# A level found in five digits of the logits' range instead of eight digits of their bits

## The chip, the core and the metric

The kernel runs on one core of one Trainium2 chip. The metric is the device time of one execution in microseconds, the median of the runs. The core has TensorE (PE, matmuls), VectorE (DVE), ScalarE (ACT), GpSimd (POOL) and SyncE (SP); each runs its own list of instructions in order and waits for the others by semaphores.

## What is computed

A gated linear recurrence, then a mixture of eight experts with balanced assignment. The reference, cut:

```python
# attention: B=4, H=8, S=768, D=48
f = 1.0 / (1.0 + np.exp(-f_logit))
for t in range(S):
    state = f[:, :, t, :, None] * state + np.einsum('bhd,bhe->bhde', k[:, :, t], v[:, :, t])
    y[:, :, t] = np.einsum('bhd,bhde->bhe', q[:, :, t], state)
# experts: x is (3072, 384), E=8, F=1024
cap = N // E                                   # 384
logits = x @ w_gate
order = np.argsort(-logits.flatten())
for idx in order:                              # the largest logit first
    tok, e = idx // E, idx % E
    if assigned[tok] >= 0 or counts[e] >= cap: continue
    assigned[tok] = e; counts[e] += 1
for e in range(E):
    mask = assigned == e
    out[mask] = np.maximum(x[mask] @ w1[e], 0.0) @ w2[e]
```

## The kernel before

**Attention.** 24 chunks of 128 positions pass through seven stages (loads and decays, gates, states, scores, outputs, transposition, gate), one chunk per stage and step. In each step DVE clips the decays (`dl`), makes `qg`, masks the scores (`am`, two predicated copies), copies `kT`, `xT` and the chunk's `logits`; POOL makes `kg`; PE's Y of a step reads the `am` of the step before. A scheduler sets the order of this part. The rows x go to `xd` in DRAM.

**Routing.** `assign_and_run` writes its order out by hand for all engines but SP. The assignment is found in seven rounds. In each, every free token takes its best open expert (`choices`: `masked`, `best`, `pick`, `taken`, `choice`), and the round looks for the highest level at which an open expert fills up. The level is searched in digits of 16 values: DVE compares each token's remainder `over` with 15 thresholds (`above`), PE counts tokens by expert and threshold (`cnt`), DVE finds the thresholds at which an expert is full (`fills`, `filled`), PE sums the digit times its unit back over all partitions, and DVE subtracts it (new `over`). The key is the logit's 32 bits in sortable form, in two halves: four digits on the high half (`high_keys`), then four on the low one (`low_keys`), with an operation between that joins them. Then `assign` takes all tokens above the level (`sure`) and, of those exactly at it (`tie`), the first ones in token order, by two more matmuls, a scan and a rank. `close` marks full experts (`penalty`, `wanted`). Each round fills an expert, and its list is made (`members`, `place`, `index`, `lines`, six `in_line`, `used`, `tokens`: twelve operations in a queue `dve_work`): `index` gives the expert's number `e` to SP, which loads its weights, and `tokens` the rows that POOL gathers from `xd` (`xe`).

**Experts.** An expert is 51 pieces of PE work in a queue `pe_work`: three `turn` (the transpositions `Xe`, copied by ACT to `xeT`), 24 `up` (`H`, with a Relu by ACT to `hT`) and 24 `down` (`O`); each finished O tile is copied by ACT and scattered to the output by POOL. `some(pe_work, n)` puts n pieces at this place of PE's order. In a search the three numbers of `pace` are the pieces ahead of the count, of the sum over groups, and of the digit's matmul: none in round 0, where there is nothing to run, (1, 1, 1) in rounds 1 and 2, (2, 1, 1) after. In rounds 1 and 2 the whole list is made right after the assignment, with one piece behind each operation; later the operations of a list are put into the next round's digits, three in each, at the places of `some(dve_work, 1)`. In round 0 `idle_turns` runs empty matmuls (`nothing`). What is left in the queue at the end runs without a break.

**A second pass.** `beyond` counts spans too long for the fast attention; every engine loads it into a register at the end, behind the last list, and if it is over zero attention and routing run once more in a slower form.

## Time and profile before

| | us |
|---|---|
| median of 3 runs | 557.81 |
| lowest and highest run | 557.68 and 567.76 |
| the profiled execution | 559.02 |
| its span | 557.1 |
| PE busy | 497.1 (89%) |
| DVE busy | 292.8 (53%) |
| ACT and POOL busy | 128.4 (23%) and 114.4 (21%) |

The span is the time from the first to the last instruction of the profiled execution. A matmul in fp32 shows as two passes in the trace, so a piece of an expert is two rows. A timeline row joins equal instructions in a row; what stands in brackets is the idle time of the engine just before and what ended it. Attention fills the first 168 us, round 0 goes on to about 209, and PE ends at 547.4.

### The profile page before, as it was taken

Reading aid. Unit: us, or ns where it says so; the run is one execution under the profiler, and the core shown is the slowest. Engines: PE = TensorE matmul, PEld = TensorE weight load, DVE = VectorE, ACT = ScalarE, POOL = GpSimd, SP = SyncE. Lnnn points to the kernel's source line nnn. Section 1 sums busy time; section 2 is a strip of 40 time slices with the busy share of each in tenths; the row PEclk is TensorE's granted clock in tenths of the full one; section 3 lists DMA queues with packets and bytes.
Section 4 is the critical chain, followed back from the end, with each engine's and each line's share of the span. In section 5 each row is a group of like instructions: output and inputs, shape, how many; then the busy total and the mean of one; then the engine's idle time right before and its main releaser. Section 6 shows DMA issues by size and latency. Waiting matters only on the chain.

```text
span 557.1 us, 12270 instructions
## 1 busy us (share of the span) xinstructions
PE 497.1 (89%) x5054; PEld 310.7 (56%) x5054; DVE 292.8 (53%) x990; ACT 128.4 (23%) x301; POOL 114.4 (21%) x172
## 2 busy tenths in 40 slices
PE   3999999999993489998997989889899989999993
PEld 2778888878873254453353545445455556556551
DVE  6566566566665664575576477377576673000000
ACT  3445554544320001101111110210111021121210
POOL 3224433422310020041013003203112143101001
PEclk9999999999995599998999999899989999999997
DMA  9878898952100070061053007107125087100000
GB/s 176 180 159 172 186 190 192 195 129 60 45 34 14 1 270 0 1 252 59 1 196 105 11 0 256 57 2 254 58 66 203 29 282 276 38 1 28 14 16 32
DMA packets 118353, 59.10 MB, mean 106 GB/s; under 512 B 101648, under 2 KB 112912, under 8 KB 118288
## 3 DMA queue, kind: packets, MB, share of 16 engines
q1 hardware_dynamic: 111760, 44.06, 29.9%
q0 software_dynamic: 3072, 9.44, 5.1%
q10 hardware_dynamic: 3456, 4.72, 2.4%
q8 instruction: 42, 0.69, 0.5%
q14 instruction: 23, 0.19, 0.1%
HBM read 48.77 MB, written 9.44 MB: 104 GB/s over the span
## 4 chain that ended last, share of the span: by engine, by line
PE 64%; issue 18%; DVE 11%; POOL 4%; DMA 1%; ACT 1%; POOLq 0%; ACTq 0%; DVEq 0%
PE H L697 17%; PE O L708 14%; PE Y L239 4%; PE T L185 4%; PE A L222 3%; PE L L153 3%; PE Y L249 2%; PE L L157 2%; PE X L265 2%; PE dS L204 2%; PE cnt L501 2%; POOL out_dram L713 2%; PE X L279 1%; PE nothing L729 1%; DMA xe<-xd,token 1%
## 5 line engine op out<-in xcount | busy, mean ns | idle before, releaser
L697 PE MATMUL H<-xeT,w 128*128 128x384 f32 x384 | 150.5, 520 | 4.2 <-ACT xeT L689 4.2
L708 PE MATMUL O<-w,hT 128*128 128x384 f32 x384 | 140.7, 504 | 0.0
L697 PEld LDWEIGHTS H<-xeT,w 128*128 128x128 f32 x384 | 68.3, 196 | 39.5 <-ACT xeT L689 5.5
L708 PEld LDWEIGHTS O<-w,hT 128*128 128x128 f32 x384 | 68.4, 191 | 36.5 <-issue 1.1
L701 ACT ACTIVATE hT<-H 128x384 f32<-128x384 f32 x64 | 31.4, 490 | 137.7 <-PE H L697 130.1
L713 POOL DMA_INDIRECT out_dram<-o,token x24 | 24.5, 1020 | 184.8 <-ACT o L712 184.2
L227 DVE COPY_PREDICATED am<-mask,A 128x512 f32<-128x512 int32 x48 | 32.4, 728 | 31.5 <-PE A L222 31.5
L712 ACT COPY o<-O 128x384 f32<-128x384 f32 x24 | 11.5, 478 | 143.3 <-PE O L708 138.0
L383 DVE TENSOR_TENSOR in_line<-line,count 128x512 bf16<-128x512 f32 x48 | 32.2, 711 | 0.2
L663 POOL DMA_INDIRECT xe<-xd,token x24 | 24.1, 1006 | 38.3 <-DVE over L383 12.9
L177 POOL TENSOR_TENSOR kg<-k,ek 128x384 f32<-128x384 f32 x24 | 25.5, 1063 | 28.5 <-ACT ek L165 22.8
L501 PEld LDWEIGHTS <-above 128*120 128x120 bf16 x144 | 13.9, 135 | 29.0 <-DVE above L383 20.8
L153 PE MATMUL L<-g,wcum 128*128 128x384 f32 x48 | 23.0, 564 | 7.9 <-DVE count L322 7.9
L239 PE MATMUL Y<-v,am 128*64 128x48 f32 x768 | 27.7, 224 | 0.0
L383 DVE TENSOR_TENSOR above<-over,steps 128x360 bf16<-128x360 f32 x49 | 26.1, 533 | 1.7
L239 PEld LDWEIGHTS Y<-v,am 128*64 128x64 f32 x768 | 24.5, 138 | 4.1 <-issue 3.7
L222 PE MATMUL A<-qT,kT 48*64 48x128 f32 x768 | 26.7, 278 | 0.0
L383 DVE TENSOR_TENSOR own<-cnt,mine 120x64 f32<-120x64 f32 x48 | 10.7, 223 | 27.8 <-PE cnt L501 27.4
L162 DVE TENSOR_SCALAR dl<-L 128x384 f32<-128x384 f32 x24 | 13.4, 558 | 20.3 <-PE L L157 20.3
L629 POOL TENSOR_TENSOR past<-b,ramp_nt 128x48 f32<-128x48 f32 x8 | 2.2, 278 | 106.2 <-DVE b L383 81.0
L501 PE MATMUL cnt<-choice,above 128*120 128x64 bf16 x144 | 15.6, 218 | 8.5 <-DVE above L383 8.5
L689 ACT COPY xeT<-Xe 128x384 f32<-128x384 f32 x24 | 10.9, 486 | 47.3 <-PE Xe L686 45.3
(164 smaller groups left out, 639.5 us busy)
## 6 DMA issues: line engine op xcount, KB each, us to landing
w<-in_moe_w_dram SPq DMA_DIRECT2D x16, 1536.0 KB, 8.5
f<-in_f_logit_dram SPq DMA_DIRECT2D x24, 192.0 KB, 4.0
q<-in_q_dram SPq DMA_DIRECT2D x24, 192.0 KB, 3.9
k<-in_k_dram SPq DMA_DIRECT2D x24, 192.0 KB, 4.4
v<-in_v_dram SPq DMA_DIRECT2D x24, 192.0 KB, 3.9
xd<-x ACTq DMA_DIRECT2D x24, 192.0 KB, 3.3
xe<-xd,token POOLq DMA_INDIRECT x24, 3.1
out_dram<-o,token POOLq DMA_INDIRECT x24, 2.6
```

The source lines that it names most:

```text
L153: nc.tensor.matmul(out=Lv, lhsT=wcum[:], rhs=g[:, :, 0:DH], start=True, stop=True)
L177: nc.gpsimd.tensor_tensor(out=kg[:, :, 0:DH], in0=G["k"][:], in1=ek[:], op=ALU.mult)
L222: nc.tensor.matmul(out=A[par][HC * j:HC * j + HC, 128 * hp:128 * hp + 128], lhsT=G["kT"][rows, hp, HC * j:HC * j + HC], rhs=G["qT"][rows, ...
L227: nc.vector.copy_predicated(am[:, par], mask[:].unsqueeze(1).to_broadcast((128, HP, 128)), A[par][:].rearrange("s (a t) -> s a t", t=128))
L239: nc.tensor.matmul(out=Y[par][HC * j:HC * j + HC, DH * hp:DH * hp + DH], lhsT=G["am"][:, par, hp, HC * j:HC * j + HC], rhs=G["v"][:, 2 * h ...
L383: nc.vector.tensor_tensor(out=out_, in0=a, in1=b, op=op)
L501: nc.tensor.matmul(out=r[0:m, 0:n], lhsT=above[:, c:c + CG].rearrange("p c n -> p (c n)"), rhs=choice[:, c:c + CG].rearrange("p c e -> p ( ...
L663: nc.gpsimd.indirect_dma_start(out=xe[:], out_offset=None, in_=xd[:, :], in_offset=bass.IndirectOffsetOnAxis(ap=token[:, i:i + 1], axis=0))
L697: nc.tensor.matmul(out=L["H"][:, 0:CAP], lhsT=L["w1"][:, d, 128 * ft:128 * ft + 128], rhs=xT[:, d, :], start=(d == 0), stop=(d == DC - 1))
L701: nc.scalar.activation(out=hT[:, ft, :], in_=L["H"][:, 0:CAP], func=AF.Relu)
L708: nc.tensor.matmul(out=L["O"][:, 0:D], lhsT=hT[:, ft, 128 * i:128 * i + 128], rhs=L["w2"][:, ft, :], start=(ft == 0), stop=(ft == FC - 1))
L713: nc.gpsimd.indirect_dma_start(out=outs[next(tiles)][:, :], out_offset=bass.IndirectOffsetOnAxis(ap=L["token"][:, i:i + 1], axis=0), in_=o ...
```

## The change

The level is no longer searched in the logit's bits but in 2^20 equal steps. Near the end of attention `bounds` takes the largest and the smallest logit of the first four of six chunks of each sequence, widens the range by an eighth on either side and makes thresholds and units for five digits from its step. `level_keys` is one operation, the logit's distance from the lower end. A round has five digits. `assign` takes all tokens at or above the level, whole steps, with no ranking of ties. If a step holds more tokens than the expert has places, `places` falls below zero; `close` keeps the lowest (`lowest`), and at the end that too sets `beyond`. The old search with its ties runs only in the second pass, which makes its own constants. `pace` after round 2 becomes (3, 2, 2). A place of a list that stays empty points at 32 rows of zeros behind `xd` (the ramps are shifted by NT for that), and the scatter leaves out rows beyond N.

```diff
+SHIFTS = (16, 12, 8, 4, 0)
...
-    xd = dram.tile([N, D], FP32, name="xd")
+    xd = dram.tile([N + 32, D], FP32, name="xd")
+    zeros = const([32, D], FP32, "zeros")
+    nc.vector.memset(zeros[:], 0.0)
...
+    nc.scalar.dma_start(out=xd[N:N + 32, :], in_=zeros[:])
...
-    nc.gpsimd.iota(out=lane_i[:], pattern=[[1, 1]], base=0, channel_multiplier=1)
+    nc.gpsimd.iota(out=lane_i[:], pattern=[[1, 1]], base=-NT, channel_multiplier=1)
...
-    ramp_nt = ramp(NT, "ramp_nt", 1, -1)
+    ramp_nt = ramp(NT, "ramp_nt", 1, -1 - NT)
...
+    def bounds(c1):
+        pair = rt([2], "pair_", FP32, 1)
+        seen = logits[:].rearrange("p (b c) e -> p b c e", b=B)[:, :, 0:c1]
+        XY = mybir.AxisListType.XYZ
+        nc.vector.tensor_reduce(out=pair[:, 0:1], in_=seen, axis=XY, op=ALU.max)
+        nc.vector.tensor_reduce(out=pair[:, 1:2], in_=seen, axis=XY, op=ALU.min)
+        ts(pair[:, 1:2], pair[:, 1:2], -1.0, ALU.mult)
+        r = ps("bounds")
+        nc.tensor.transpose(out=r[0:2, 0:128], in_=pair[:], identity=ident[:])
+        top, tops = rt([1], "top", FP32, 1), rt([2], "tops", FP32, 1)
+        reduce(top[0:2, :], r[0:2, 0:128], ALU.max)
+        ts(tops[0:2, :], ident[0:2, 0:2], top[0:2, :], ALU.mult)
+        nc.tensor.matmul(out=r[:, 128:130], lhsT=two[0:2, :], rhs=tops[0:2, :], start=True,
+                         stop=True)
+        ends, width = rt([2], "ends", FP32, 1), rt([1], "width", FP32, 1)
+        nc.vector.tensor_copy(out=ends[:], in_=r[:, 128:130])
+        reduce(width[:], ends[:], ALU.add)
+        stt(lowlogit[:], width[:], -0.125, ends[:, 1:2], ALU.mult, ALU.subtract)
+        short, step = rt([1], "short", BF16, 1), rt([1], "step", FP32, 1)
+        ts(short[:], width[:], 1.25 / 2 ** 20, ALU.mult, 1e-30, ALU.max)
+        nc.vector.tensor_copy(out=step[:], in_=short[:])
+        for shift in SHIFTS:
+            steps = const([128, NTH], FP32, f"steps_{shift}")
+            ts(steps[:], count[:, 0:NTH], step[:], ALU.mult, float(1 << shift), ALU.mult)
+            unit = const([128, 128], BF16, f"unit_{shift}")
+            ts(unit[:], ones[:], step[:], ALU.mult, -float(1 << shift), ALU.mult)
+            digits.append((steps, unit))
+    def level_keys(best, over):
+        ts(over, best, lowlogit[:], ALU.max, lowlogit[:], ALU.subtract)
...
-            high_keys(best[:], of(key), half[:], of(high))
+            level_keys(best[:], of(over))
...
-        def search(choice, over, slots):
-            for shift, slots in zip((12, 8, 4, 0), slots):
+        def search(choice, over, digits, slots):
+            for steps, unit in digits:
...
         def assign(choice, over, slots):
+            sure = rt([NT, E], "sure", BF16)
+            stt(sure[:], col(over[:], E), 0.0, choice[:], ALU.is_ge, ALU.mult)
+            count = rt([E], "count", BF16)
+            with nc.allow_low_precision("counts of at most 24"):
+                reduce(count[:], by_e(sure), ALU.add)
+            some(pe_work, slots[0])
+            r = bank("sums", "r")
+            nc.tensor.matmul(out=r[:, 0:E], lhsT=ones[:], rhs=count[:], start=True, stop=True)
+            some(pe_work, slots[1])
+            tt(assigned[:], assigned[:], sure[:], ALU.add)
+            tt(places[:], places[:], r[:, 0:E], ALU.subtract)
+            ts(full[:], places[:], 0.5, ALU.is_lt)
+        def assign_exact(choice, over, slots):
+            after, notfirst, _ = exact
...
         def close():
             ts(penalty[:], full[:], CLOSED, ALU.mult)
+            tt(lowest[:], lowest[:], places[:], ALU.min)
...
-                nc.vector.tensor_copy(out=pair[:].rearrange("p a n -> p (a n)"), in_=r[:, 0:2 * TE])
+                ts(pair[:].rearrange("p a n -> p (a n)"), r[:, 0:2 * TE], float(NT), ALU.add)
...
-                            in_=o[:], in_offset=None)
+                            in_=o[:], in_offset=None, bounds_check=N - 1, oob_is_err=False)
...
-                low = rt([NT], "low")
-                low_keys(key[:], low[:])
-                slots = [pace.get(rnd, (2, 1, 1))] * 4
-                over = search(choice, high, slots)
-                stt(over[:], over[:], 65536.0, low[:], ALU.mult, ALU.add)
-                over = search(choice, over, slots)
+                slots = pace.get(rnd, (3, 2, 2))
...
+                        level_keys(best[:], over[:])
+                    over = search(choice, over, digits, slots)
...
             if again is not None:
+                worst = rt([1], "worst")
+                reduce(worst[:], lowest[:], ALU.min)
+                stt(beyond[:], worst[0:1, :], -0.5, beyond[:], ALU.is_lt, ALU.max)
                 again.append(nc.values_load(beyond[0:1, 0:1], min_val=0, max_val=128))
...
-    attention(6, ALL - 4)
+    attention(6, ALL - 8)
+    bounds(NCH - 2)
+    attention(ALL - 8, ALL - 4)
...
-        assign_and_run(None)
+        assign_and_run(exact=exact_constants())
```


**PE in round 3, from one digit's count to the next.** `cnt` are the search's matmuls, O the pieces of an expert, numbers in names the buffers. Before:

```order
L501 MATMUL cnt<-choice,above 120x64
L708 MATMUL O<-w_4009,hT 128x384
L513 LDWEIGHTS pick_th
L513 MATMUL cnt<-part,pick_th 15x8
L708 MATMUL O<-w_4009,hT 128x384
L535 LDWEIGHTS unit_538
L535 MATMUL cnt<-filled,unit_538 128x1
L708 MATMUL O<-w_4009,hT 128x384 x2
L501 LDWEIGHTS above
L501 MATMUL cnt<-choice,above 120x64
```

After:

```order
L551 MATMUL cnt<-choice,above 120x64
L775 MATMUL O<-w_3822,hT 128x384 x2
L563 LDWEIGHTS pick_th
L563 MATMUL cnt<-part,pick_th 15x8
L775 MATMUL O<-w_3822,hT 128x384 x2
L585 LDWEIGHTS unit_2666
L585 MATMUL cnt<-filled,unit_2666 128x1
L775 MATMUL O<-w_3822,hT 128x384 x3
L551 LDWEIGHTS above
L551 MATMUL cnt<-choice,above 120x64
```

Two pieces stand where one stood, and three where two stood, around the same search matmuls.

**DVE in the attention step in which the bounds are made**, from `dl` on. Before:

```order
L162 TENSOR_SCALAR dl<-L 128x384
L167 COPY spans<-L 128x8
L281 COPY logits<-X 128x8
L268 COPY xT<-X 128x384
L176 TENSOR_TENSOR qg_94<-q,eq 128x8x48
L227 COPY_PREDICATED am_99<-mask,A 128x512 x2
```

After:

```order
L170 TENSOR_SCALAR dl<-L 128x384
L175 COPY spans<-L 128x8
L406 TENSOR_REDUCE top<-bounds 2x1
L289 COPY logits<-X 128x8
L400 TENSOR_SCALAR tops<-ident,top 2x2
L184 TENSOR_TENSOR qg_96<-q,eq 128x8x48
L436 COPY ends<-bounds 128x2
L276 COPY xT<-X 128x384
L406 TENSOR_REDUCE width<-ends 128x1
L403 SCALAR_TENSOR_TENSOR lowlogit<-width,ends 128x1
L400 TENSOR_SCALAR short<-width 128x1
L442 CAST step<-short 128x1
```

Behind the last row shown follow `steps` and `unit`, five times each, and then the two `am` that closed the rows of before.

**PE at the end of round 4**, from the last digit's last count to the pieces ahead of the next round's first count. `Xe` are the transpositions of the gathered rows. Before:

```order
L513 MATMUL cnt<-part,pick_th 15x8
L697 MATMUL H<-xeT,w_4777 128x384
L535 LDWEIGHTS unit_546
L535 MATMUL cnt<-filled,unit_546 128x1
L549 LDWEIGHTS ones
L549 MATMUL sums<-tie,ones 128x192
L550 LDWEIGHTS after
L550 MATMUL sums<-tie,after 128x192
L697 MATMUL H<-xeT,w_4777 128x384
L557 LDWEIGHTS ones
L557 MATMUL sums<-count,ones 128x8
L697 MATMUL H<-xeT,w_4777 128x384 x10
```

After:

```order
L563 LDWEIGHTS pick_th
L563 MATMUL cnt<-part,pick_th 15x8
L775 MATMUL O<-w_4095,hT 128x384 x2
L585 LDWEIGHTS unit_2674
L585 MATMUL cnt<-filled,unit_2674 128x1
L753 MATMUL Xe<-ident,xe 128x128 x3
L602 LDWEIGHTS ones
L602 MATMUL sums<-count,ones 128x8
L753 MATMUL Xe<-ident,xe 128x128 x6
L764 MATMUL H<-xeT,w_4441 128x384 x9
```

The two `sums<-tie` are gone, and the transpositions of expert 3, which stood two digits earlier, now stand around the count's matmul.

## Rows read from the trace of the kernel before

**Rows 1.** The page, granted clock of PE in 40 slices of 13.9 us.

```profile
PEclk9999999999995599998999999899989999999997
```

**Rows 2.** Timeline of PE: start us, us, engine, line, operation, count [idle before, releaser].

```profile
481.26 1.15 PE L686 MATMUL Xe<-ident,xe 128*128 128x128 f32 x9
483.18 15.75 PE L697 MATMUL H<-xeT,w 128*128 128x384 f32 x48 [0.78 <-ACT xeT L689]
...
514.25 1.15 PE L686 MATMUL Xe<-ident,xe 128*128 128x128 f32 x9
```

**Rows 3.** Timeline of DVE, round 0.

```profile
171.61 0.18 DVE L383 TENSOR_TENSOR over<-high,cnt 128x24 f32<-128x24 f32 x1 [0.25 <-PE cnt L535]
...
173.78 0.18 DVE L383 TENSOR_TENSOR over<-over,cnt 128x24 f32<-128x24 f32 x1 [0.25 <-PE cnt L535]
...
187.30 0.36 DVE L390 SCALAR_TENSOR_TENSOR tie<-over,choice 128x192 bf16<-128x192 f32 x1
...
188.71 0.16 DVE L383 TENSOR_TENSOR places<-places,sums 128x8 f32<-128x8 f32 x1
...
191.31 0.16 DVE L383 TENSOR_TENSOR score<-left,full 128x8 f32<-128x8 f32 x1
```

**Rows 4.** Timeline of PE, two digits of round 1.

```profile
212.62 0.35 PE L501 MATMUL cnt<-choice,above 128*120 128x64 bf16 x3
...
215.59 0.35 PE L501 MATMUL cnt<-choice,above 128*120 128x64 bf16 x3
```

**Rows 5.** Timeline of PE, two digits of round 3.

```profile
317.44 0.30 PE L501 MATMUL cnt<-choice,above 128*120 128x64 bf16 x3
...
320.84 0.30 PE L501 MATMUL cnt<-choice,above 128*120 128x64 bf16 x3
```

**Rows 6.** The page, groups: line, engine, operation, busy us and mean ns, idle before.

```profile
L383 DVE TENSOR_TENSOR in_line<-line,count 128x512 bf16<-128x512 f32 x48 | 32.2, 711 | 0.2
```

**Rows 7.** Timeline of PE, end of round 2.

```profile
276.53 0.17 PE L535 MATMUL cnt<-filled,unit 15*128 15x1 bf16 x1
277.37 0.50 PE L549 MATMUL sums<-tie,ones 128*128 128x192 bf16 x1 [0.67 <-DVE tie L390]
...
278.72 4.12 PE L697 MATMUL H<-xeT,w 128*128 128x384 f32 x12
```

**Rows 8.** Timeline of PE, start of round 3.

```profile
296.90 0.35 PE L501 MATMUL cnt<-choice,above 128*120 128x64 bf16 x3 [2.94 <-DVE above L383]
```

**Rows 9.** Waits from 205 to 560: who waited for whom, us, times, longest.

```profile
PE cnt L501 <- DVE above L383: 8.5, 7, 3.6
...
PE cnt L513 <- DVE part L393: 1.9, 4, 0.7
```

**Rows 10.** Timeline of PE, round 4.

```profile
345.54 0.76 PE L653 MATMUL tokens<-number,in_line 128*128 128x6 bf16 x24
...
350.13 0.55 PE L686 MATMUL Xe<-ident,xe 128*128 128x128 f32 x3 [0.38 <-DMA xe<-xd,token]
...
357.51 0.30 PE L501 MATMUL cnt<-choice,above 128*120 128x64 bf16 x3
```

**Rows 11.** Timeline of PE, end of round 5 and start of round 6.

```profile
402.10 8.08 PE L697 MATMUL H<-xeT,w 128*128 128x384 f32 x15 [0.56 <-ACT xeT L689]
...
411.63 0.30 PE L501 MATMUL cnt<-choice,above 128*120 128x64 bf16 x3
```

**Rows 12.** Busy us of each engine in one stretch, granted clock.

```profile
402.00:405.00 3.00, 2.90 (x5) 1.68 (x6) 2.89 (x10) 0.05 (x1) 0.00 (x0) 0.50 0.02 5
```

**Rows 13.** Timeline of DVE, attention.

```profile
140.88 1.35 DVE L227 COPY_PREDICATED am<-mask,A 128x512 f32<-128x512 int32 x2 [1.56 <-PE A L222]
```

**Rows 14.** Timeline of PE, attention.

```profile
143.82 1.14 PE L239 MATMUL Y<-v,am 128*64 128x48 f32 x32
```

**Rows 15.** Timeline, last list: DVE's expert number and SP's DMA.

```profile
459.04 0.14 DVE L387 TENSOR_SCALAR e<-m 128x1 int32<-128x1 f32 x1
...
459.73 0.37 SPq L610 DMA_DIRECT2D w<-in_moe_w_dram  x1
```

More of the change, by code (lines that the diff above doesn't have):

```diff
@@ L309 @@
     nc.vector.memset(ones[:], 1.0)
-    after = const([128, 128], BF16, "after")
-    nc.vector.tensor_tensor(out=after[:], in0=ltri[:], in1=ones[:], op=ALU.subtract)
     onesf = const([128, 1], FP32, "onesf")
     nc.vector.memset(onesf[:], 1.0)
+    two = const([2, 128], FP32, "two")
+    nc.vector.memset(two[:], 1.0)
     onesc = const([128, NT], FP32, "onesc")
@@ L333 @@
     first = ramp(E, "first", -1, E + 1)
-    steps, units = {}, {}
-    for shift in (12, 8, 4, 0):
-        steps[shift] = ramp(NTH, f"steps{shift}", 1 << shift, 0)
-        units[shift] = const([128, 128], BF16, f"unit{shift}")
-        nc.vector.memset(units[shift][:], -float(1 << shift))
     mine8 = const([128, CG, E], FP32, "mine8")
@@ L359, with exact_constants @@
     nc.vector.memset(idle[:], 1.0)
-    notfirst = const([128, E, NT], FP32, "notfirst")
-    nc.vector.memset(notfirst[:], 1.0)
-    nc.vector.memset(notfirst[:, :, 0:1], 0.0)
+    def exact_constants():
+        after = const([128, 128], BF16, "after")
+        nc.vector.tensor_tensor(out=after[:], in0=ltri[:], in1=ones[:], op=ALU.subtract)
+        notfirst = const([128, E, NT], FP32, "notfirst")
+        nc.vector.memset(notfirst[:], 1.0)
+        nc.vector.memset(notfirst[:, :, 0:1], 0.0)
+        digits = []
+        for shift in (12, 8, 4, 0):
+            unit = const([128, 128], BF16, f"unit{shift}")
+            nc.vector.memset(unit[:], -float(1 << shift))
+            digits.append((ramp(NTH, f"steps{shift}", 1 << shift, 0), unit))
+        return after, notfirst, digits
     def col(t, *shape):
@@ L401 @@
     assigned = rt([NT, E], "assigned", BF16, 1)
+    lowest = rt([E], "lowest", FP32, 1)
+    lowlogit, digits = const([128, 1], FP32, "lowlogit"), []
+    def bounds(c1):
[27 more added lines that the diff above has]
+        ts(over, best, lowlogit[:], ALU.max, lowlogit[:], ALU.subtract)
     outs = dram_disjoint_views(out, NT)
@@ L424, in begin @@
         nc.vector.memset(assigned[:], 0.0)
-        choice = rt([NT, E], "choice", BF16)
-        key, high = rt([NT], "key", I32), rt([NT], "high")
+        nc.vector.memset(lowest[:], 0.0)
+        choice, over = rt([NT, E], "choice", BF16), rt([NT], "over")
         def part(c0, c1):
@@ L438, in over_e @@
                 return t.unsqueeze(3).to_broadcast((128, B, n, E))
-            best, pick, half = rt([B, n], "best0"), rt([B, n], "pick0"), rt([B, n], "half0", I32)
+            best, pick = rt([B, n], "best0"), rt([B, n], "pick0")
             masked = rt([B, n, E], "masked0")
@@ L448, in part, with assign_and_run @@
             tt(of_e(choice), masked[:], over_e(pick[:]), ALU.is_equal)
-        return (choice, key, high), part
-    def assign_and_run(begun, also=None, again=None):
+        return (choice, over), part
+    def assign_and_run(begun=None, also=None, again=None, exact=None):
         stack = ExitStack()
@@ L514, in counts_beside @@
             return cnt
-        def search(choice, over, slots):
-            for shift, slots in zip((12, 8, 4, 0), slots):
+        def search(choice, over, digits, slots):
+            for steps, unit in digits:
                 above = rt([NT, NTH], "above", BF16)
-                tt(above[:], col(over[:], NTH), row(steps[shift][:], NTH), ALU.is_ge)
+                tt(above[:], col(over[:], NTH), row(steps[:], NTH), ALU.is_ge)
                 r = bank("cnt", "r")
@@ L534, in search @@
                 digit = r[:, 128:129]
-                nc.tensor.matmul(out=digit, lhsT=units[shift][0:NTH, :],
+                nc.tensor.matmul(out=digit, lhsT=unit[0:NTH, :],
                                  rhs=filled[0:NTH, :], start=True, stop=True)
@@ L646, in used @@
                 used = rt([E], "used")
-                tt(used[:], left[:], L["sel"][:], ALU.mult)
+                stt(used[:], left[:], 1.0, L["sel"][:], ALU.add, ALU.mult)
                 tt(left[:], left[:], used[:], ALU.subtract)
@@ L883 @@
             nc.sync.dma_start(
-                out=xd[:, :].rearrange("(b c t) d -> b t c d", b=B, c=NCH)[
+                out=xd[0:N, :].rearrange("(b c t) d -> b t c d", b=B, c=NCH)[
                     bass.ds(b, 1)].rearrange("b t c d -> (b t) c d"),
```

26 lines of the change are left out of this document (17 added, 9 removed).

## The prediction

> **What bounds the kernel now.** I read the slices first, then the PE row of the timeline from the end backwards, then the waits of PE round by round. PE's clock falls to half for two slices in the middle [rows 1]; there lies round 0 of the routing, where PE has nothing to do but count and the chain runs through DVE. After it PE works through eight experts. One expert takes 514.25 − 481.26 = 32.99 us for its 51 pieces, and one piece (two matmul passes of 384 columns) takes 15.75/24 = 0.656 us [rows 2]. From the count at 212.62 [rows 4] to the end of the last expert, one such stretch behind 514.25, are 334.6 us; the pieces that are left there need some 260. The missing 74 are counts of the search, waits at the ends of rounds and stretches at the lower clock. They lie on the path one for one: PE's order is fixed, so every microsecond that it loses moves the last expert. Each edit is therefore priced in PE time after round 0, and in DVE time in round 0.
>
> **Round 0.** A digit lasts 173.78 − 171.61 = 2.17 us [rows 3], with DVE and PE in turn and nothing beside them. Three of eight go: 6.5. The operation that joins the key's halves goes: 0.2, like `over` in the same rows. Ahead of the first `above` four operations on keys and two on the low half give way to one; half of them lay in the shadow of others, so I take 0.5. The assignment took 191.31 − 187.30 = 4.01 from `tie` to `score`. Of it remain `sure`, `count`, the count's matmul and `places` (188.71 − 187.30 = 1.41 less about 0.3 for `tie`) and then `full` and the step to `score`, 0.4: 1.5, a gain of 2.5. Sum 9.7. What follows (list, idle turns, gather) is unchanged and moves forward whole.
>
> **Rounds 1 and 2, the digits.** A digit has three pieces and lasts 215.59 − 212.62 = 2.97 [rows 4]; the pieces are 1.97, so the digit itself costs PE 1.00. The pieces not run here run later at 0.656 each, so only that cost counts: 3 digits × 2 rounds × 1.00 = 6.0.
>
> **Rounds 3 to 6, the digits.** Four pieces, 320.84 − 317.44 = 3.40 [rows 5], less 2.62: 0.78. With seven pieces in a digit the same three breaks cost the same 0.78 as long as DVE keeps up. It does: in rounds 1 and 2 DVE got through a digit and the waits in it within 2.97; 7 × 0.656 + 0.78 = 5.4 leave 2.4, and the three list operations of a digit are 0.71 at most, the mean of `in_line` [rows 6]. 3 × 4 × 0.78 = 9.4.
>
> **The assignment on PE.** From the last digit's matmul to the pieces behind the count: 278.72 − 276.53 = 2.19, less one piece, 1.53 [rows 7]. PE waited 0.67 for `tie` and ran two matmuls of 192 columns. Now the count's matmul comes after `over`, `sure` and `count`: 0.84 as for `tie`, and one reduction more at about 0.5, 1.4 with its own 0.17 about 1.6; less the piece 0.95. Gain 0.58 × 6 = 3.5.
>
> **The ends of rounds.** PE waited seven times for `above`, 8.5 us in all: 3.6 between rounds 1 and 2, 2.94 between 2 and 3, and 2.0 in five others; and 1.9 for `part` in four [rows 8, 9]. The long ones are DVE's run from `penalty` to the first `above`. Six small operations leave it and two come (`over`, `lowest`), at 0.2: −0.8 for each, and one more piece of cover (0.66) ahead of round 3. In the later rounds DVE also loses the whole tie part behind the count, some 2.5 us, and PE has eleven pieces as cover where it had ten: of the 3.9 of short waits I count 2.6 as gone, and leave the rest, which stand beside transpositions or at the old pace. 0.8 + 1.5 + 2.6 = 4.9.
>
> **Where the gathers land.** In round 4 the pieces of expert 2 ran out four after `tokens` of expert 3, and PE stood for its gather and lost speed: from `tokens` on 357.51 − 345.54 = 11.97 instead of 0.7 for `tokens`, 1.3 for two pieces and 6.8 for two digits, 3.1 lost [rows 10]. By the new pace 146 of 153 pieces are done when that list is finished (2 + 36 + 36 + 44 + 28), so seven are left: with the digit around them 6 us, against the 4.6 us from `tokens` (345.54) to the first transposition (350.13) in the same rows. The stall goes: 3.1. But the three transpositions now fall on the assignment of round 4, and those of expert 1 on that of round 2. The same meeting in round 5 of the kernel before was followed by ten pieces in 411.63 − 402.10 = 9.53 instead of 6.56 [rows 11], at granted clock 0.50, which is the 1.2 GHz level [rows 12]: 2.97 lost. One such dip disappears and I expect one in two of the new places: net 0. The range holds none and two. The dip after the wait of 3.6 may go as well, since none followed the 2.94; I leave that to the range.
>
> **What it adds.** `bounds` puts three operations where DVE idles 1.56 ahead of `am` [rows 13], which costs nothing, and one step later some sixteen (the ends, the step, ten for steps and units) ahead of the next `am`. At 0.2 to 0.25 they are 3.5, of which 1.56 is idle time, so `am` ends 2 us late, at 144.2 for a Y that begins at 143.82 [rows 14]; `dl`, and through ACT and POOL the next `kg`, are as late. Of the two `bounds` matmuls the first stands ahead of PE's X and the second inside Y, and DVE's `ends`, which waits for the second, holds back `xT`, which the next step's X needs; there is a step of slack for that. PE loses between 0.5 (am alone) and 3.5 (nothing absorbed); no end below nothing, since only work comes there. I take 1.5, nearer to the `am`. At the end every engine's load of `beyond` waits for the last list: behind `tokens` PE has one piece, 0.66, while DVE does four operations, about 1.0, and a load follows; from the end of `e` to the DMA that uses it on SP 459.73 − 459.18 = 0.55 go by [rows 15]. 1.0 + 0.55 − 0.66 = 0.9, between 0 (the load runs ahead, as it did) and 1.5. Behind it on PE are the last 130 pieces, so it counts in full; on ACT two Relu, on POOL the last scatters stand behind theirs, and on SP nothing, since its load moved behind the last weights. The bounds check of the scatters lies off the path except for the last one: 0 to 1, taken as 0. The write of the zero rows stands first in ACT's queue, under the first loads; the shifted ramps and the constants lie there too: 0.
>
> **The sum.** 9.7 + 6.0 + 9.4 + 3.5 + 4.9 + 3.1 − 1.5 − 0.9 = 34.2. The profiled execution took 559.02, so 524.8; it stood 1.2 above the median of the runs, 557.81. Forecast 523.6.
>
> **Rivals.**
> *The second pass is taken.* If one step holds the token that fills an expert and another one of that expert, places falls below −0.5, the register is set and attention and routing run again: at least the 385 us from the first digit of round 0 [rows 3] to the end of the span once more, over 940 in all. It decides at a step of 1.25 × 0.1285 / 2^20 = 1.5e-7. From the reference's own logits, at each of the seven levels the next token of that expert lies at least 104 steps below. Chance 0.02. This is the case on the other side.
> *The clock dips in every round.* Each round still breaks PE's stream; if each is followed by a dip of 2.97, six instead of one cost 14.9 more: 538. For it: three stretches below full clock after round 0 in the kernel before [rows 1]. Against: the wait of 2.94 was not followed by one. The Trainium skill (TensorE: Matmul & The Clock Gate, "A second HAM failure mode: psum-queue depth-cycling") says that an engine which idles briefly and often between groups of matmuls can swing between its two clock levels and lose throughput each time; by that rule it is this case, and the trace agrees only in part, since half of the rounds stayed at full clock. Chance 0.08.
> *The lists become the bound.* Their twelve operations now fall on four digits of five. If PE then waits 0.67 in each of twelve digits, as it did for `tie`, and the stall of rows 10 stays, 8.0 + 3.1 more: 535. Against: the 2.4 us that a longer digit leaves to DVE. Chance 0.08.
> *Only round 0 gains.* If the breaks cost PE as much in five long digits as in eight short ones, the 15.4 of the digits stay: 539. Rows 4 and 5 speak against it, 1.00 with three pieces and 0.78 with four. Chance 0.05.
> *Attention pays more*, 5 us and a dip of its own: 530. Chance 0.03. Two of these together, the clock and the digits, give 554, with 0.02.
>
> **How the numbers follow.** The forecast has 0.72. Its own range: down by 3.0 (no new dip), 2.97 (the dip after the wait of 3.6 gone), 2.4 (the added costs nothing) and 1.3 (the rest of the short waits) to 514; up by 3.0 (two dips) and 3.6 (the three added costs at their upper ends) to 530. To hold 8 in 10 it goes on to 535, which takes in the attention case and the lists. Two per cent, 11 us, is about what a measurement of this kernel can tell from no change: below 546.6 are all cases but the double one and the second pass, so 0.96, 0.02 and 0.02.
>
> **What would show it.** From the first digit's `over` to the first list's `score` about 10.5 us instead of 19.7; five digits per round; 0.8 to 1.0 per digit beyond its pieces; no wait for `xe` near the fourth list; waits of some 2.8 and 1.5 ahead of rounds 2 and 3 and none ahead of 4 to 6; a pause of about 1 us behind the last `tokens`; an attention step near 143 longer by 1 to 2 us. I am wrong if PE's time per digit grows with its pieces, if the clock falls in most rounds, or if the register sends the program round again.

## The result, and the profile after

| | before | changed |
|---|---|---|
| median, us (4 runs each) | 561.26 | 517.98 |
| lowest and highest run | 557.68 and 567.76 | 514.78 and 519.59 |
| the profiled execution, its span | 559.02, 557.1 | 514.78, 513.0 |
| last count's input ready: last X of attention | 167.44 | 166.89 |
| first count of round 1 | 209.09 | 198.78 |
| end of PE | 547.40 | 503.09 |

The ratio is 0.924, 95% interval 0.914 to 0.935: faster, and 5.6 us below the forecast of 523.6. One of the four runs before, 567.76, is over 1.5% above the fastest and does not enter the ratio. The medians differ by 43.3. The two profiled executions differ by 44.2, where the sum said 34.2.

The profile of the changed kernel is that of the run of 514.78, with a mean granted clock of 0.978. The other three, of which there is no trace, had 0.975 (516.58), 0.972 (519.37) and 0.972 (519.59): somewhere they ran longer at the lower level.

The page of the changed kernel, granted clock in 40 slices of 12.8 us:

```profile
PEclk9999999999999679999999999999999999999997
```

Beside [rows 1] the low stretch of round 0 is still there, and no slice between it and the last is below 9. In this execution, that is the first thing that the prediction did not have.

**Round 0**, timeline of DVE (the same columns as [rows 3]):

```profile
177.07 0.18 DVE L396 TENSOR_TENSOR over<-over,cnt 128x24 f32<-128x24 f32 x1 [0.25 <-PE cnt L585]
...
179.25 0.18 DVE L396 TENSOR_TENSOR over<-over,cnt 128x24 f32<-128x24 f32 x1 [0.25 <-PE cnt L585]
179.47 0.36 DVE L403 SCALAR_TENSOR_TENSOR sure<-over,choice 128x192 bf16<-128x192 f32 x1
...
180.63 0.16 DVE L396 TENSOR_TENSOR places<-places,sums 128x8 f32<-128x8 f32 x1
...
181.03 0.17 DVE L396 TENSOR_TENSOR score<-left,full 128x8 f32<-128x8 f32 x1
```

A digit lasts 179.25 − 177.07 = 2.18, as before. From `sure` to `score` are 1.56 us; from `tie` to `score` they were 4.01 [rows 3]. `score` stands at 181.03 instead of 191.31: 10.28, of which 0.55 is the earlier end of attention, so the round itself gained 9.73.

**Digits and assignment**, timeline of PE: two digits of round 1, the assignment of round 1, two digits of round 3:

```profile
202.31 0.35 PE L551 MATMUL cnt<-choice,above 128*120 128x64 bf16 x3
...
205.28 0.35 PE L551 MATMUL cnt<-choice,above 128*120 128x64 bf16 x3
...
213.17 0.17 PE L585 MATMUL cnt<-filled,unit 15*128 15x1 bf16 x1
...
214.53 0.18 PE L602 MATMUL sums<-count,ones 128*128 128x8 bf16 x1 [0.35 <-DVE count L406]
214.57 6.05 PE L764 MATMUL H<-xeT,w 128*128 128x384 f32 x18
...
269.59 0.30 PE L551 MATMUL cnt<-choice,above 128*120 128x64 bf16 x3
...
274.93 0.30 PE L551 MATMUL cnt<-choice,above 128*120 128x64 bf16 x3
```

Three pieces and a digit take 2.97, as in [rows 4]. A digit with seven pieces takes 5.34; less 7 × 0.656 that is 0.75, against 0.78 with four [rows 5]. So the price of a digit does not grow with what is packed into it. From the last digit's matmul to the pieces behind the count are 1.40, less one piece 0.74; before it was 1.53 [rows 7].

**Waits.** PE from 197 to 425, who waited for whom (us in total, times, longest), and then the timeline of PE at the starts of rounds 2 and 3 and around the transpositions that meet an assignment:

```profile
PE cnt L551 <- DVE above L396: 4.3, 2, 2.8
...
PE cnt L563 <- DVE part L406: 0.3, 1, 0.3
```

```profile
231.92 0.35 PE L551 MATMUL cnt<-choice,above 128*120 128x64 bf16 x3 [2.76 <-DVE above L396]
...
246.71 0.18 PE L602 MATMUL sums<-count,ones 128*128 128x8 bf16 x1 [0.72 <-DVE count L406]
...
264.20 0.35 PE L551 MATMUL cnt<-choice,above 128*120 128x64 bf16 x3 [1.52 <-DVE above L396]
...
322.43 0.55 PE L753 MATMUL Xe<-ident,xe 128*128 128x128 f32 x3
323.69 0.17 PE L602 MATMUL sums<-count,ones 128*128 128x8 bf16 x1 [0.71 <-DVE count L406]
...
325.19 6.07 PE L764 MATMUL H<-xeT,w 128*128 128x384 f32 x18 [0.62 <-ACT xeT L756]
```

The two long waits are 2.76 and 1.52, forecast as 2.8 and 1.5; the short ones of [rows 9] are gone but for 0.3; no wait for `xe` is left. The transpositions stand at the assignments of rounds 2 and 4, where they were expected, and the piece row behind them (18 passes in 6.07) runs at full speed.

**What was added**, timeline of PE in attention and at the last list, and of DVE between the ten constants and `am`:

```profile
132.00 1.07 PE L230 MATMUL A<-qT,kT 48*64 48x128 f32 x32
136.04 0.27 PE L429 MATMUL bounds<-ident,pair__2636 128*2 128x128 f32 x1
...
138.23 0.38 PE L433 MATMUL bounds<-tops,two 2*128 2x2 f32 x2
...
139.28 1.07 PE L230 MATMUL A<-qT,kT 48*64 48x128 f32 x32
...
417.43 0.89 PE L764 MATMUL H<-xeT,w 128*128 128x384 f32 x2
418.81 1.53 PE L764 MATMUL H<-xeT,w 128*128 128x384 f32 x4 [0.49 <-issue]
```

```profile
139.81 0.23 DVE L400 TENSOR_SCALAR steps<-count,step 128x15 f32<-128x15 f32 x1
139.96 0.25 DVE L400 TENSOR_SCALAR unit<-ones,step 128x128 bf16<-128x128 bf16 x1
...
141.32 1.34 DVE L235 COPY_PREDICATED am<-mask,A 128x512 f32<-128x512 int32 x2
```

From A to A are 7.28 us. `am` ended at 142.66, ahead of its Y, since the ten constants follow each other 0.15 apart though each is listed with 0.23 or 0.25. Behind the last list PE loses 418.81 − 417.43 − 0.66 = 0.7.

### The profile page after: what moved, and what is told of

Same layout as the page of the kernel before. It is cut to its first block, busy times and chain, and to the rows that moved or that the text cites. A ratio compares the mean times of both kernels' runs of the same rounds, so it can differ in the third digit from the quotient of the medians.

```text
span 513.0 us, 11743 instructions
## 1 busy us (share of the span) xinstructions
PE 465.9 (91%) x4878; PEld 299.8 (58%) x4878; DVE 243.7 (48%) x797; ACT 127.9 (25%) x301; POOL 111.3 (22%) x172
## 4 chain that ended last, share of the span: by engine, by line
PE 67%; issue 18%; DVE 8%; POOL 3%; ACT 1%; DMA 1%; POOLq 0%; ACTq 0%; DVEq 0%
PE H L764 17%; PE O L775 16%; PE Y L247 5%; PE T L193 4%; PE A L230 4%; PE L L161 4%; PE L L165 3%; PE Y L257 2%; PE X L273 2%; PE dS L212 2%; POOL out_dram L780 2%; PE X L287 2%; PE nothing L796 2%; PE cnt L551 1%; ACT xeT L756 1%
## 5 line engine op out<-in xcount | busy, mean ns | idle before, releaser
L764 PE MATMUL H<-xeT,w 128*128 128x384 f32 x384 | 137.4, 499 | 5.1 <-ACT xeT L756 4.6
L775 PE MATMUL O<-w,hT 128*128 128x384 f32 x384 | 137.6, 498 | 0.0
L165 PEld LDWEIGHTS L<-ind,g 128*64 128x64 f32 x384 | 13.5, 141 | 13.6 <-issue 13.6
L230 PEld LDWEIGHTS A<-qT,kT 48*64 48x64 f32 x768 | 20.8, 133 | 0.2
L172 ACT ACTIVATE eq<-dl 128x384 f32<-128x384 f32 x24 | 12.5, 522 | 28.3 <-DVE dl L170 27.8
L396 DVE TENSOR_TENSOR above<-over,steps 128x360 bf16<-128x360 f32 x35 | 18.7, 533 | 1.2
```

What stands on the lines that cost most here:

```text
L165: nc.tensor.matmul(out=ends[DP * r:DP * r + DP, :, hp], lhsT=g[:, 2 * hp + r, :], rhs=ind[:], start=True, stop=True)
L230: nc.tensor.matmul(out=A[par][HC * j:HC * j + HC, 128 * hp:128 * hp + 128], lhsT=G["kT"][rows, hp, HC * j:HC * j + HC], rhs=G["qT"][rows, ...
L396: nc.vector.tensor_tensor(out=out_, in0=a, in1=b, op=op)
L764: nc.tensor.matmul(out=L["H"][:, 0:CAP], lhsT=L["w1"][:, d, 128 * ft:128 * ft + 128], rhs=xT[:, d, :], start=(d == 0), stop=(d == DC - 1))
L775: nc.tensor.matmul(out=L["O"][:, 0:D], lhsT=hT[:, ft, 128 * i:128 * i + 128], rhs=L["w2"][:, ft, :], start=(ft == 0), stop=(ft == FC - 1))
```

## The experiments

All are compared by one account, so that only what PE does not spend on pieces is left. For each round I take the time from its first count to that of the next (in round 6, to the end of PE) and subtract 0.656 [rows 2] for each piece that lies in between; for round 0 the time from attention's last X. Round 1 of the changed kernel: 231.92 − 198.78 = 33.14, less 36 × 0.656 = 23.62, leaves 9.52. Between the first counts of rounds 2 and 3 lie 38 pieces, since the new pace puts three and not one ahead of the first count of round 3; behind that of round 6 lie 199.

| profiled execution | last X | round 0 | 1 | 2 | 3 | 4 | 5 | 6 to the end |
|---|---|---|---|---|---|---|---|---|
| before | 167.44 | 41.65 | 14.35 | 13.76 | 8.46 | 13.18 | 12.39 | 10.47 |
| changed | 166.89 | 31.89 | 9.52 | 7.35 | 4.09 | 5.09 | 4.97 | 7.61 |
| changed, again | 167.40 | 31.75 | 9.77 | 7.30 | 4.09 | 5.51 | 4.97 | 7.59 |
| eight digits | 169.90 | 37.93 | 12.56 | 12.27 | 6.88 | 12.49 | 7.23 | 10.27 |
| ties back | 169.27 | 34.24 | 10.61 | 9.83 | 4.89 | 7.22 | 5.77 | 8.41 |
| pace back | 169.48 | 31.81 | 9.80 | 7.96 | 5.03 | 5.88 | 5.41 | 8.94 |
| waits filled | 167.75 | 31.70 | 7.17 | 6.89 | 4.15 | 5.03 | 4.94 | 6.98 |
| four digits | 170.57 | 29.27 | 8.54 | 9.36 | 2.91 | 8.33 | 3.79 | 7.61 |
| range given | 167.19 | 31.91 | 9.79 | 8.73 | 4.08 | 5.61 | 4.98 | 7.60 |
| four digits, filled | 167.84 | 30.05 | 5.93 | 5.55 | 3.35 | 5.39 | 4.46 | 7.16 |

| kernel | median, us (runs) | ratio to before, interval |
|---|---|---|
| changed, again | 518.42 (4) | 0.925, 0.917 to 0.934 |
| eight digits | 547.4 (4) | 0.981, 0.976 to 0.986 |
| ties back | 527.7 (4) | 0.946, 0.941 to 0.952 |
| pace back | 522.08 (6) | 0.935, 0.931 to 0.938 |
| waits filled | 512.58 (5) | 0.918, 0.914 to 0.922 |
| four digits | 516.45 (4) | 0.919, 0.911 to 0.926 |
| range given | 517.84 (4) | 0.923, 0.915 to 0.930 |
| four digits, filled | 508.26 (4) | 0.905, 0.898 to 0.912 |
| second pass | 5033.16 (1) | none, one run |

The kernel before had a median of 558.77 beside eight digits, ties back, pace back and waits filled, and of 563.88 beside the other four. So a difference of some 5 us between medians of the two groups, or to the first 517.98, can come from the occasion; where it matters the account decides.

**Eight digits.** Three empty digits are put in front of the five, at the old pace; the ties stay out.

```diff
-SHIFTS = (16, 12, 8, 4, 0)
+SHIFTS = (28, 24, 20, 16, 12, 8, 4, 0)
-                slots = pace.get(rnd, (3, 2, 2))
+                slots = pace.get(rnd, (2, 1, 1))
```

> The changed kernel with three more digits on top (shifts 28, 24 and 20, whose thresholds no token reaches, so the level found is the same) and the old pace (2, 1, 1); range, whole steps and assignment stay as changed. Theory (a digit has its price wherever it stands): 3 x 2.17 in round 0, 3 x 1.0 in each of rounds 1 and 2, 3 x 0.76 in each of rounds 3 to 6, so 6.5 + 6 + 9.1 = 21.6 us more than the changed kernel's 515 to 520, and as the pieces are again 4 short of the fourth list the stall there (3 us) and perhaps a dip: 537 to 546. Rival (the gain came from where gathers and transpositions land and from the clock, the digits being hidden): no more than 8 us over the changed kernel, 523 to 528, with the digit's cost on PE the same in the trace but given back in shorter waits.

547.4: 29.4 of the 43.3 that the medians gained go back, and the time is 1.4 above the range expected. Round 0 pays 6.0, round 1 3.0, rounds 3 and 5 2.8 and 2.3. Round 2 pays 4.9: its first wait, 2.79, was followed by a clock of 0.66 from 250 to 255, and one piece less covers the wait ahead of round 3, 2.15. Round 4 pays 7.4, since the stall of [rows 10] is back. Timeline of PE in that round:

```profile
343.41 0.55 PE L753 MATMUL Xe<-ident,xe 128*128 128x128 f32 x3 [0.74 <-DMA xe<-xd,token]
344.71 0.55 PE L753 MATMUL Xe<-ident,xe 128*128 128x128 f32 x3 [0.75 <-DMA xe<-xd,token]
...
347.08 1.65 PE L764 MATMUL H<-xeT,w 128*128 128x384 f32 x2 [0.46 <-ACT xeT L756]
```

Two passes take 1.65 where 0.91 is usual: the lower clock level follows the three waits, as it did before.

**Ties back.** `assign_exact` in all rounds, five digits.

```diff
+    ties = exact_constants()
-                (assign_exact if exact else assign)(choice, over, (1, 8))
+                assign_exact(choice, over, (1, 8))
```

> The changed kernel with only the assignment as before (ties ranked by two matmuls, a scan and a rank in every round). Theory: 2.5 us in round 0, 0.6 to 0.8 us of PE in each of six rounds, and in the rounds from 4 on the cover of 11 pieces (7.2 us) still hides DVE's longer tail, so only the waits ahead of rounds 2 and 3 stay as they are: 2.5 + 4.2 = 7 us more, 522 to 527. Rival (PE's assignment is hidden since the pieces behind it wait for other things anyway): only round 0's 2.5, 517 to 522.

527.7, 9.7 more and 0.7 above the range expected. Round 0 pays 2.35 (2.5 was forecast for the assignment there), rounds 1, 3 and 5 between 0.8 and 1.1, rounds 2 and 4 2.5 and 2.1. In this execution the clock fell in both of these, behind the wait of 3.05 ahead of round 2 (0.81 from 236 to 241) and behind the transpositions that meet the assignment in round 4 (0.72 from 332 to 338); the changed kernel's profile has neither dip, so not all of the 9.7 is the ranking. The two stretches (us, PE busy and instructions, granted clock, DMA share, GB/s); the page's slices are printed with the next experiment's:

```profile
236.00:241.00 5.00, 3.26 (x10) 0.81 0.43 118
332.00:338.00 6.00, 5.16 (x17) 0.72 0.20 66
```

**Pace back.** Five digits, no ties, the old (2, 1, 1) after round 2.

```diff
-                slots = pace.get(rnd, (3, 2, 2))
+                slots = pace.get(rnd, (2, 1, 1))
```

> The changed kernel with the old pace (2, 1, 1) in five digits. Theory (pieces not run in the search run later at the same price): same time within 2 us; 0.75 to 0.8 us per digit beyond its pieces, though a digit of 3.4 us may leave DVE short of time in the digits that carry three list operations, up to 0.6 us in each of four such digits in three rounds: 515 to 523. Rival (the pace brought part of the gain): 5 to 10 us more, 522 to 528.

522.08, 4.1 more. The expectation held and its rival's range touches it, so the median does not decide. The account does: round 4 costs 5.88 and PE did not stand for `xe` there. So at the old pace eight digits have the stall and five do not. In all the old pace costs 4.3: 0.6 in round 2, 0.9, 0.8 and 0.4 in rounds 3 to 5, and 1.3 in round 6. Two waits of PE grew, by 0.6 and 0.9: ahead of round 3, where one piece less covers DVE (2.12 for 1.52), and for the last list's `e` (2.35 for 1.49). Behind each the clock was 0.66 for five microseconds (267 to 272, 376 to 381). By an estimate from the 1.4 that such a dip cost in the experiment with the range given (below), the two waits and the two dips come to 4.3. That leaves nothing for the pieces that run later, as the theory had it. Timeline of PE at the two waits:

```profile
266.94 0.35 PE L551 MATMUL cnt<-choice,above 128*120 128x64 bf16 x3 [2.12 <-DVE above L396]
...
376.61 0.16 PE L667 MATMUL before<-total,ltri 128*128 128x1 bf16 x1 [2.35 <-DVE e L400]
```

The page's clock, ties back first, pace back second:

```profile
PEclk9999999999999579998999999899999999999997
```

```profile
PEclk9999999999999679999989999999989999999997
```

**Waits filled.** Four pieces ahead of round 2's first count and two ahead of round 3's, taken from the later digits.

```diff
-                slots = pace.get(rnd, (3, 2, 2))
+                slots = pace.get(rnd, (2, 2, 2))
...
+                        some(pe_work, {2: 4, 3: 2}.get(rnd, 0))
                         over = search(choice, over, digits, slots)
```

> The changed kernel with four pieces put ahead of round 2's first count and two ahead of round 3's, where PE waited 2.76 and 1.52 us, and pace (2, 2, 2) so that the pieces last until the fourth gather. Theory (PE's waits lie on the path one for one): 4.2 us less, 511 to 516. Rival (the waits are only moved, to the gather or to DVE, which comes later by what it loses): within 1 us of the changed kernel, 515 to 520.

512.58, 5.4 below the changed kernel and within the theory's range. By the account it is 3.7: rounds 1 and 2 give 2.35 and 0.5, round 6 gives 0.6, and nothing is paid back later. Timeline of PE at the two waits:

```profile
232.86 0.35 PE L551 MATMUL cnt<-choice,above 128*120 128x64 bf16 x3 [0.44 <-issue]
...
265.33 0.35 PE L551 MATMUL cnt<-choice,above 128*120 128x64 bf16 x3 [0.83 <-DVE above L396]
```

The wait of 2.76 fell to 0.44, that of 1.52 only to 0.83: the pace (2, 2, 2) takes one piece from ahead of round 3's first count where the edit puts two. No dip follows in this profile. The rest of the 5.4 is not shown: it may be dips that runs of the changed kernel have, or the occasion.

**The changed kernel again.**

> The changed kernel once more, nothing edited. It asks which parts of its profile belong to the kernel and which to the execution. Theory: the start of attention varies by 1 to 3 us from one execution to the next, since the last X of attention stood at 166.89 in the changed kernel's profile, at 167.44 in that of before, and at about 169.3 to 169.9 in three experiments that edited nothing in attention; then the median is 515 to 520 again, the last X lies anywhere from 166.9 to 170, and everything behind it keeps its distances (first digit to first score 10.5, round 1's first count 18 behind the score), with no stretch at the 1.2 GHz level after round 0. Rival: the dips vary too; then this profile shows one or two slices at 8 or less after round 0, as the experiment with the ties back did, and its span is 2 to 4 us longer than attention's shift explains.

518.42 beside 517.98. Last X and rounds 0 to 6 agree with the first profile within 0.5, and no slice between round 0 and the last is below 9. Again the profiled run is the one with the highest mean clock of the four: 0.978 (515.58), 0.976 (516.92), 0.971 (519.93) and 0.970 (522.22). So for the profiled run the rival is wrong; for the others it is open, and their clocks speak for it, since the profile with one dip (range given) has a mean of 0.975 and pace back's, with two, 0.971.

The forecast of 1 to 3 us for attention's spread is not borne out by this pair, but by the others: with the same attention code the last X stood at 169.27 to 170.57 in four executions of edited kernels. The late ones lose it partly behind the first steps: in eight digits PE waited 0.84 for `kg` at 116.82, because POOL had waited 2.28 for a load of `f`.

**The range given.** The ends of the range are constants; finding them in the logits is left out.

```diff
+        nc.vector.memset(lowlogit[:], -0.0741)
+        width = rt([1], "width", FP32, 1)
+        nc.vector.memset(width[:], 0.12849)
...
     begun, part = begin()
+    bounds(NCH - 2)
-    attention(6, ALL - 8)
-    bounds(NCH - 2)
-    attention(ALL - 8, ALL - 4)
+    attention(6, ALL - 4)
```

> The range's lower end and width are constants, so the reductions over the logits, the transposition, the small matmul and the copies of the bounds are left out, and the ten operations for steps and units stand at the start of the program; finding the range in the logits is the part of the computation that this leaves out. Theory (the bounds cost attention about 0.85 of PE time, as the distance between the two traces between the A of two steps says): 517.1, not to be told from 518 in the medians, and PE's A, Y and X of the steps near 131 to 145 as far apart as in the kernel before. Rival (they cost the 1.5 to 3.5 of a stalled am and its followers): 514.5 to 516.5, with a gap ahead of Y in the changed kernel that is gone here.

517.84: no difference to be seen in medians, as the theory said. The trace has it, PE in attention and the start of round 2; the last row is the changed kernel's repetition at the same wait:

```profile
133.14 1.07 PE L230 MATMUL A<-qT,kT 48*64 48x128 f32 x32
...
139.58 1.07 PE L230 MATMUL A<-qT,kT 48*64 48x128 f32 x32
...
232.51 0.35 PE L536 MATMUL cnt<-choice,above 128*120 128x64 bf16 x3 [3.03 <-DVE above L396]
...
235.09 1.65 PE L760 MATMUL O<-w,hT 128*128 128x384 f32 x2
```

```profile
232.54 0.35 PE L551 MATMUL cnt<-choice,above 128*120 128x64 bf16 x3 [3.01 <-DVE above L396]
```

A to A is 6.44 again, so `bounds` costs 7.28 − 6.44 = 0.84. And in this run the clock fell after the wait ahead of round 2, with the routing code unchanged. The same stretch in three executions (the stretch, us, PE busy and instructions, granted clock, DMA share, GB/s): the changed kernel, its repetition, the range given:

```profile
232.00:237.00 5.00, 5.00 (x21) 1.00 0.19 58
```

```profile
232.00:237.00 5.00, 4.46 (x18) 1.00 0.27 79
```

```profile
232.00:237.00 5.00, 4.49 (x15) 0.69 0.29 79
```

Waits of 2.76, 3.01 and 3.03 stand at this place; only the last was followed by a dip, and its round 2 costs 8.73 instead of 7.3: 1.4.

**Four digits.** 2^16 steps.

```diff
-SHIFTS = (16, 12, 8, 4, 0)
+SHIFTS = (12, 8, 4, 0)
-        ts(short[:], width[:], 1.25 / 2 ** 20, ALU.mult, 1e-30, ALU.max)
+        ts(short[:], width[:], 1.25 / 2 ** 16, ALU.mult, 1e-30, ALU.max)
-                slots = pace.get(rnd, (3, 2, 2))
+                slots = pace.get(rnd, (3, 3, 3))
```

> The range is taken as 2^16 steps instead of 2^20, so a round has four digits; pieces in a digit (3,3,3) after round 2, so that a round of four digits runs 36 pieces where five ran 35. Theory (a digit costs what the traces showed: 2.18 in round 0, 0.97 beyond its pieces in rounds 1 and 2, 0.75 in rounds 3 to 6): 2.2 + 1.9 + 3.0 = 7.1 less, 511 (508 to 514) beside 518 for the changed kernel. Rival (the lists need the fifth digit: twelve operations now fall on four digits, and each digit's breaks get longer, or transpositions and assignment meet at a new place and the clock dips): rounds 3 to 6 gain nothing, one dip of 3 is added, 514 to 518.

516.45, 2.0 below the changed kernel where 7.1 was expected: the rival's range; the ratios' intervals overlap, and the account has 0.7. Rounds 0, 1, 3 and 5 gave 2.6, 1.0, 1.2 and 1.2, as priced or better; rounds 2 and 4 took back 2.0 and 3.2. Timeline of PE ahead of rounds 2 and 5, then the stretch behind the first:

```profile
230.03 0.51 PE L551 MATMUL cnt<-choice,above 128*120 128x64 bf16 x3 [2.78 <-DVE above L396]
...
325.24 0.55 PE L753 MATMUL Xe<-ident,xe 128*128 128x128 f32 x3 [0.79 <-DMA xe<-xd,token]
326.50 0.55 PE L753 MATMUL Xe<-ident,xe 128*128 128x128 f32 x3 [0.71 <-DMA xe<-xd,token]
327.61 5.18 PE L764 MATMUL H<-xeT,w 128*128 128x384 f32 x10 [0.57 <-ACT xeT L756]
```

```profile
230.00:235.00 5.00, 4.97 (x11) 0.50 0.30 102
```

The wait is 2.78, like the 2.76 that passed without a dip, and 5 us at the 1.2 GHz level follow. In round 4 the list ends so late in four digits that its gather is waited for (0.18, 0.79, 0.71), and a clock of 0.72 from 326 to 332 follows. So the fifth digit was not idle time: part of what leaving it out saves is given back at the lists.

**Four digits, waits filled.**

```diff
-                slots = pace.get(rnd, (3, 2, 2))
+                slots = pace.get(rnd, (3, 3, 2))
...
+                        some(pe_work, {2: 4, 3: 2}.get(rnd, 0))
```

(with the three lines of four digits above)

> Four digits, and besides the waits ahead of the first counts of rounds 2 and 3 filled with 4 and 2 pieces; pieces in a digit (3,3,2) after round 2. Theory (both edits save what they save alone: 5.4 by the medians for the filled waits, 7.1 for the digits): 505.5 (503 to 509). Rival (the two save the same time, since with fewer pieces used in digits the later rounds have more left and the waits cost less, or the run without a break at the end grows and nothing is saved there): 509 to 513.

508.26: the fastest, within the theory's range, 10.2 below the changed kernel's repetition on the same occasion and 4.3 below the filled waits alone; the ratios' intervals touch in neither pair. The starts of rounds 2 and 3:

```profile
228.09 0.35 PE L551 MATMUL cnt<-choice,above 128*120 128x64 bf16 x3 [0.21 <-DVE above L396]
...
257.91 0.35 PE L551 MATMUL cnt<-choice,above 128*120 128x64 bf16 x3 [0.18 <-DVE above L396]
```

Waits of 0.2 are left, and no slice between round 0 and the last is below 9. By the account the two edits give 1.8 in round 0, 3.6 and 1.8 in rounds 1 and 2, 1.4 behind them, 8.6 in all: more than the 3.7 and the 0.7 that each gives alone, since this profile has neither of the dips of four digits, and less than the 12.5 of the theory's sum. A gather in round 4 is still waited for, 0.75. Its steps are sixteen times as wide, so by the reference's logits the nearest rival of a level is 6.5 steps away instead of 104.

**The second pass forced.** The register is set whatever the places are.

```diff
-                stt(beyond[:], worst[0:1, :], -0.5, beyond[:], ALU.is_lt, ALU.max)
+                stt(beyond[:], worst[0:1, :], 1.0e9, beyond[:], ALU.is_lt, ALU.max)
```

> The threshold on the lowest number of places is set so that the register always sends the program round again; the output is the exact pass's. It prices the rival on the other side. Theory (the prediction's lower bound): at least the 385 us of the routing and the experts once more behind a first pass of 518, and attention in its slower form, over 940 in all. Rival (the second pass costs only its routing and experts, because its attention is short beside them): 900 to 940.

5033 us. The page, groups (line, engine, operation, busy us and mean ns, idle before):

```profile
L934 DVE TENSOR_TENSOR_SCAN stc<-fc,kv 128x768 f32<-128x768 f32 x768 | 1536.9, 2001 | 1268.0 <-PE Y L939 1266.5
```

The scan of the slower attention runs 768 times, about 5.1 us apart (1999.18 to 2004.30 in the timeline): 3.9 ms of the 4.5 that the pass adds. "Over 940" was a true bound, but five times too low to weigh the rival by: at 4.5 ms one pass in a hundred launches would cost the gain of 43 each.

## Why the prediction was right, and where its sizes were off

The mechanism held: PE's order is fixed, each microsecond that it does not spend on pieces moves the end, and the account by rounds gives back the 44 (43.8, and 0.55 of attention). Its terms, forecast and measured in the profiled execution:

| term | forecast | measured | from |
|---|---|---|---|
| round 0 | 9.7 | 9.7 | `score` against `score` |
| digits, rounds 1 and 2 | 6.0 | 6.0 | 2.97 and 2.97 |
| digits, rounds 3 to 6 | 9.4 | 10.0 | 4 × (8 × 0.78 − 5 × 0.75) |
| assignment on PE | 3.5 | 4.7 | 6 × (1.53 − 0.74) |
| long waits | 2.3 | 2.2 | 3.58 and 2.94 to 2.76 and 1.52 |
| short waits | 2.6 | 3.6 | 3.9 to 0.3 |
| stall of round 4 | 3.1 | 3.5 | the round's 13.18 − 5.09, less 2.5 for digits, 0.8 for the assignment, 1.3 of short waits |
| dips | 0 | 4.2 | 2.97 of round 5; 1.2 behind the wait of 3.58, see below |
| `bounds` | −1.5 | −0.8 | A to A |
| load of `beyond` | −0.9 | −0.7 | pause behind the last list |
| first loads of attention | none | 1.3 | see below |

The measured terms sum to 43.7 of 44.2. **The digits** were the largest part and right in mechanism: a digit's breaks cost 0.75 to 1.0 whatever lies in them; eight digits put back 29.4, the stall and a dip among them, and pace back shows that at the old pace five digits have no stall. **The ties** cost 9.7 alone, with two dips in the profile; the sum had 2.5 in round 0 and 3.5 on PE for them, and their share of the ends of rounds. The assignment on PE gave 1.2 more than forecast: the count's matmul came 1.36 behind the last digit's, where 1.4 and its own 0.17 were taken, and the pieces follow it by 0.04.

**The step that was mis-sized** is "One such dip disappears and I expect one in two of the new places: net 0." The transpositions came where it said, with waits of 0.72, 0.71 and 0.62, and no dip followed in either profile of the changed kernel; ties back had one at the same meeting in round 4. It took the dip for a property of the place, at one in two. The runs show it as something an execution has or has not: of eleven waits of 2 to 3.6 us behind rounds 1 and 2 in the ten profiles six are followed by ten microseconds at a mean clock of 0.69 to 0.83, and five by a clock of 1.00, in no order of length (2.94 and 3.01 without, 2.12 and 2.78 with); of five waits of about 1.5 none is. The Trainium skill (TensorE: Matmul & The Clock Gate, "A second HAM failure mode: psum-queue depth-cycling") has the engine swing between its levels when it idles often between groups of matmuls. The runs agree that such breaks can be followed by the lower level, at 1.4 to 3 us each, and show that it does not follow every one.

So part of the 4.2 is luck of the two executions that were profiled: the one before held three stretches below full clock behind round 0, the changed one none. By an estimate from the mean clocks of the other three runs of the changed kernel (0.972 to 0.975, where the profiles with one and two dips have 0.975 and 0.971) these held one or two, though no trace shows where, and the median lies 3.2 above the profiled run.

The dip behind the longest wait of the kernel before, which the prediction left to its range, went as well: the digit after it lasted 256.79 − 252.96 = 3.83 instead of 2.97 and the transposition in the next one 0.88 instead of 0.55, 1.2 in all. Timeline of PE before:

```profile
252.96 0.35 PE L501 MATMUL cnt<-choice,above 128*120 128x64 bf16 x3 [3.58 <-DVE above L383]
...
256.79 0.46 PE L501 MATMUL cnt<-choice,above 128*120 128x64 bf16 x3
257.06 0.88 PE L686 MATMUL Xe<-ident,xe 128*128 128x128 f32 x3
```

**Attention.** "At 0.2 to 0.25 they are 3.5" used the listed duration of small operations; start to start they take 0.15, so `am` was on time and only PE's own matmuls cost. The 1.3 of the first loads belongs to these two executions: the second A began at 23.40 in the changed kernel and at 24.94 before, and the A ahead of `bounds` at 132.00 and 133.32, while that A stood at 132.51 in the repetition and at 133.14 with the range given.

**The rivals.** The lists become the bound did not happen with five digits, but with four it did in round 4, and cost 3.2 there with the dip behind it. The clock in every round (538) did not happen; two dips in one execution are the most that a profile of five digits showed. Only round 0 gains is refuted by rounds 1 to 5. The second pass did not run; its price stands above.

## What to carry to other kernels

Where one engine's order is fixed and full, price a change by the breaks that it puts into that order and subtract the work in between: such an account, round by round, held to half a microsecond between two executions of the same kernel. Fill the longest waits with work from later on, even where that work is not on the critical path there: in the two kernels that do so the longest wait went and no dip stood there in the profile, and with it one digit less paid 4.3 instead of 2.0. Look at the clock of every run before a profile without a dip is taken for the kernel: here the profiled run had the highest of four, twice. A guard that sends the program to a slow exact path needs its price measured, not bounded, and a margin to match.

## What was unexpected of the hardware

The same instructions with the same wait (3.01 and 3.03 us) kept the granted clock at 1.00 in one execution and fell to 0.69 over 5 us in another. The end of attention lay between 166.89 and 170.57 with no edit in its steps but `bounds`. DVE's small operations on 128x15 and 128x128 are listed with 0.23 and 0.25 us and start 0.15 apart.
